# Retention attention and a cosine-gated feed-forward layer on one core: the tile of rows 1024 to 1535 computes its second layer directly, and the seven block products begin one tile later

## The chip, the cores and the metric

The kernel runs on one core of a Trainium2 chip. The metric is the device time of one execution in microseconds (us), lower is better; the time given for a kernel is the median of its runs. A profile is one execution taken by the hardware profiler, and its span reaches from the first to the last instruction.

The core has five engines, each with an instruction stream of its own that it works through in order: PE is TensorE (matmuls; PEld is its weight load), DVE is VectorE, ACT is ScalarE, POOL is GpSimd, SP is SyncE. SP issues nearly all the DMA transfers of this kernel; SPq in a profile is that queue.

## The reference

```python
# q, k, v: (8, 8, 576, 64) float32: batch, head, position, head dimension
scores = scale * np.matmul(q, k.transpose(0, 1, 3, 2))
gamma = 1.0 - 2.0 ** (-5.0 - np.arange(H, dtype=np.float32))
Dmat = np.where(rel >= 0, gamma[:, None, None] ** rel[None, :, :], 0.0)   # rel = i - j
attn = np.matmul(scores * Dmat[None, :, :, :], v)

x = attn.transpose(0, 2, 1, 3).reshape(4608, 512)      # one row per token
h = x @ w_in             # 512 -> 2048
g = h * np.cos(h)
out = g @ w_out          # 2048 -> 512, float32
```

A causal attention without softmax, whose weights decay with the distance, then a two-layer feed-forward block with the activation h·cos(h).

## The kernel before

**Groups and tiles.** The 4608 rows are 36 groups of 128 rows (`NG`), nine to every two batches. The feed-forward layers work on ten tiles: `widths = [512, 256, 256] + [512] * 7`. Tile 0 is rows 0 to 511, tiles 1 and 2 are 256 rows each, tile 3 is rows 1024 to 1535 (groups 8 to 11), tile 9 is the last.

**A group's way.** `load(g)` issues the DMAs of q, k and v on SyncE (tiles fq, fk, fv, five buffers each). `prep(g)` scales q and k by powers of gamma into `qks` and casts v into `vb`: three instructions on GpSimd (lines 140 and 156; for groups above 25 the cast is ScalarE's). `transposes(g)` issues on SyncE a transposing DMA from `qks` to `qkT` (line 167). On TensorE, `scores` makes the products of k and q within the group (line 195), and VectorE multiplies them by the causal mask (line 207). Groups of one batch are tied by a state: `states([g, g+1])` adds their products of k and v (lines 266, 285, 287), and `attn_out` joins the masked scores times v with q times the state (lines 319, 333); ScalarE copies the result into the tile's `xT` (line 350). `scores2(g)` is the scores of g and g+1, in the PSUM banks a and b. `unit(g, ...)` and `unit7(g, ...)` are the states of g+1 and g+2, the output of g and g+1, and, if `more`, `scores2(g+2)`. So a unit asks for `prep` of up to g+3 and for the transposes of g+2 and g+3.

**The first layer.** `mm1` makes one block of 1024 PSUM columns: the matmuls (line 365), the cosine on ScalarE (line 373), the product on VectorE into the bf16 tile `gT` (line 374). A tile of 512 rows has eight blocks, in the banks a, b and m. `gT` has one buffer.

**The second layer, directly.** `mm2` makes 128 rows at a time with 16 matmuls of 128x512 (line 382); ScalarE copies the result (line 392), SyncE stores it. Tiles 0 to 2 do this. `todo` lists which attention work is put in ahead of which matmul.

**The second layer by seven products.** From tile `S7` on, `gT` is taken as two by two blocks (the halves of its rows and of its 16 column tiles), as is `w_out`. Seven products of sums of blocks (112 matmuls of 128x256, line 517) replace eight of blocks. The sums of `w_out` are made once by `w_sums` on VectorE (line 418); those numbered 3 and 4 are made in place in `w_out_sb`, so they can only follow the last direct use of it, and stand in tile `S7`'s first layer. The sums of `gT` are `g_sum` (line 445): sum 5 on VectorE, the others on GpSimd, two column tiles an instruction, with some exceptions in tile `S7` and in the last tile. The products go in the order 3, 4, 5, 2, 1, 7, 6. Products 3 and 4 need no sum of `gT`. `at` says which unit stands ahead of which product, and `late_sums` emits the second half of the sums within the unit ahead of product 4.

**The order of instructions.** It is written by hand: each engine works through its instructions in the order in which the program emits them. What feeds the attention is ordered by `feed(s)`, called with the store of group s of the output (in `mm2` after each 128 rows; in `mm2_seven` after products 5, 2, 7 and 6). `feed` emits `prep`, `transposes` and `load` for later groups. Before tile `S7` it has a loop with these limits:

```python
while prepared < min(loaded, 2 * s + 7, s + 11, starts[S7] // P + 8):
    prep(prepared)
```

From tile `S7` on, with n the tile's number after `S7` and r the store's number in the tile:

```python
while prepared < min(NG, starts[S7] // P + 10 + 4 * n + ((0, 1, 2, 4) if n else (-1, 0, 1, 4))[r]):
    prep_next()
```

With `S7 = 3` this gives, as GpSimd and SyncE get it: groups up to 15 by s = 5; group 16 among the sums of tile 3, group 17 at s = 9, 18 at s = 10, 19 to 21 at s = 11; 22 at s = 13, 23 at s = 14, 24 and 25 at s = 15; and so on, four groups a tile, of which the last two come with its last store.

The functions that the change touches, and what calls them:

Of the kernel before, what the change touches and what calls it, by code (L numbers as in the profile page):

```python
# [17 lines left out]
def kernel(  # L18
# [16 lines left out]
    nc = tc.nc  # L35
    P = 128
# [7 lines left out]
    NG = NTOK // P  # L44
# [9 lines left out]
    assert sum(widths) == NTOK  # L54
    starts = [sum(widths[:n]) for n in range(len(widths))]
    N_PE_T = 6
    S7 = 3
    LD = 5

    consts = ctx.enter_context(tc.tile_pool(name="consts", bufs=1))  # L60
# [70 lines left out]
    def prep(g, early=False, kv_first=False):  # L131

        c = g % PER
        fk, fv = (tiles.pop(("f" + n, g)) for n in "kv")
        qks = nat.tile([P, 2, H, D], BF16, tag="qks", name="qks")
        vb = nat.tile([P, H, D], BF16, tag="vb", name="vb")
        qkT = trp.tile([P, 2 * HG, P], BF16, tag="qkT", name="qkT")

        def scaled(eng, m, f, by):
            eng.tensor_tensor(  # L140
                out=qks[:, m].rearrange("p (b a) d -> p a b d", a=2),
                in0=f.rearrange("p (a b) d -> p a b d", a=2),
                in1=by[:, c, :].rearrange("p (a b) -> p a b", a=2).unsqueeze(3).to_broadcast(
                    [P, 2, HG, D]
                ),
                op=ALU.mult,
            )

        if not early and not kv_first:
            scaled(nc.gpsimd, 0, tiles.pop(("fq", g)), gq)  # L150
        scaled(nc.vector if g == 3 else nc.gpsimd, 1, fk, gk)
        if early:
            tiles["fv", g] = fv
        else:
            copy_v = nc.scalar.copy if g > starts[S7] // P + 17 else nc.gpsimd.tensor_copy
            copy_v(vb, fv)  # L156
            if c == MIX and g > PER:
                copy_v(v_odd[HP:, g // PER % 2], fv[HP:])
        if kv_first:
            scaled(nc.gpsimd, 0, tiles.pop(("fq", g)), gq)  # L160
        qT = qT4[:, :, g * P : (g + 1) * P] if early else qkT[:, :HG, :]
        tiles["a", g] = (qks, vb, qkT, qT)
# [213 lines left out]
    def mm2(n, tsi, et):  # L376
        gT = tiles["g", n]
        if et == 0:
            bank = {0: "nmnm", 1: "nm", 2: "mn"}[n][tsi]
            tiles["o", tsi] = psum.tile([P, DM], F32, tag=bank, name="o")  # L380
        ps = tiles["o", tsi]
        nc.tensor.matmul(  # L382
            ps,
            lhsT=gT[:, et, tsi * P : (tsi + 1) * P],
            rhs=w_out_sb[:, et, :],
            start=(et == 0),
            stop=(et == ET - 1),
        )
        if et == ET - 1:
            s = starts[n] // P + tsi  # L390
            ot = op.tile([P, DM], F32, tag="oabcd"[1 + s % 4], name="ot")
            nc.scalar.copy(ot, ps)  # L392
            nc.sync.dma_start(out[s * P : (s + 1) * P, :], ot)
            feed(s)

    E2 = ET // 2
# [28 lines left out]
    def g_sum(n, x, e0, e1):  # L425

        gT = tiles["g", n]
        a, b, op_ = {
            5: ((0, 0), (0, 1), ALU.add),
            2: ((1, 0), (1, 1), ALU.add),  # L430
            1: ((0, 0), (1, 1), ALU.add),
            7: ((0, 1), (1, 1), ALU.subtract),
            6: ((1, 0), (0, 0), ALU.subtract),
        }[x]
        if ("gs", n, x) not in tiles:
            tiles["gs", n, x] = sump.tile([P, E2, 256], BF16, tag=f"gs{x}", name=f"gs{x}")
        on_dve = x == 5 or (n, x) == (S7, 2) or (n, x, e0) in (
            (S7, 1, 4), (last, 1, 0), (last, 2, 4)
        )
        step = e1 - e0 if on_dve else 2  # L440
        for e in range(e0, e1, step):
            i0, i1 = (
                gT[:, k * E2 + e : k * E2 + e + step, r * 256 : (r + 1) * 256] for r, k in (a, b)
            )
            i = (nc.vector if on_dve else nc.gpsimd).tensor_tensor(  # L445
                out=tiles["gs", n, x][:, e : e + step], in0=i0, in1=i1, op=op_
            )
            if on_dve:
                tiles["gate"] = i
            elif "gate" in tiles:  # L450
                tc.add_manual_dep(
                    i.ins,
                    tiles.pop("gate").ins.name,
                    mybir.DependencyInfo(mybir.DependencyClass.Sync, mybir.DependencyReason.DATA),
                    reason="port free",
                )

    def sums_after(n, i):

        if n == S7:  # L460
            if i < 4:
                w_sums(3 + i % 2, i // 2 * 4, i // 2 * 4 + 4)
            elif i < 6:
                g_sum(n, 5, i % 4 * 4, i % 4 * 4 + 4)
                if i == 5:
                    g_sum(n, 6, 0, 4)
            elif i == 7:
                g_sum(n, 2, 0, E2)
                g_sum(n, 1, 4, E2)
                g_sum(n, 1, 0, 4)  # L470
                for e in (0, 4):
                    g_sum(n, 7, e, e + 4)
                prep_next(kv_first=True)
                g_sum(n, 6, 4, E2)
        elif n == S7 + 1 and i in (3, 7):
            for x in (5, 2, 1):
                g_sum(n, x, i - 3, i + 1)
            for x in (7, 6) if i == 7 else ():
                for e in (0, 4):
                    g_sum(n, x, e, e + 4)  # L480
        elif i == 3:
            for x in (5, 2, 1, 7, 6) if n < last else (5, 1, 2, 7, 6):
                g_sum(n, x, 0, 4)
        elif i == 7 and n == last:
            late_sums(n)
# [113 lines left out]
    def feed(s):  # L599
# [2 lines left out]
        before = loaded  # L602
        n, r = divmod(s - starts[S7] // P, 4)
        if n >= 0:
            while prepared < min(NG, starts[S7] // P + 10 + 4 * n + ((0, 1, 2, 4) if n else (-1, 0, 1, 4))[r]):
                prep_next()
            while transposed < prepared:
                transposes(transposed)
                transposed += 1
            ahead = starts[S7] // P + 14 if n == 0 and r < 3 else prepared + LD  # L610
            while loaded < min(NG, prepared + LD, ahead):
                load(loaded)
                loaded += 1
            return
# [165 lines left out]
    for n, w in enumerate(widths):  # L780
# [8 lines left out]
        else:  # L789
            m = 1024 // w  # L790
            blocks = [(et, 0, w) for et in range(0, ET, m)]
            if n > S7:
                blocks = [(e + k * E2, 0, w) for e in range(0, E2, m) for k in range(2)]
        banks = {0: "abmabmab", 1: "bmba", 2: "bmab", 3: "mamabmab"}.get(n, "abmabmab")
        for i, (et, c0, cw) in enumerate(blocks):
# [27 lines left out]
        elif n == 2:  # L823
            todo = [(11, lambda: scores2(g)), (25, lambda: unit(g, "m", soon=True))]
            late += [lambda: unit(g + 2, "b", False)]
        else:
            at = {}
            if n + 1 < len(widths):
# [1 line left out]
                    4: lambda then, off: unit7(g, "st", True, lambda: late_sums(n), off),  # L830
                    1: lambda then, off: unit7(g + 2, "n", True, then),
                }
                if n in (3, 4):
                    at = {
                        5: lambda then, off: (then(), scores2(g)),
                        1: lambda then, off: unit7(g, "n", True, then),
                        6: lambda then, off: unit7(g + 2, "b", n > 3, then),
                    }
            mm2_seven(n, at)
            continue  # L840
        todo.sort(key=lambda u: u[0])
# [42 lines left out]
```

## Time and profile before

| | us |
|---|---|
| runs | 300.07, 300.51, 303.6 |
| median | 300.51 |
| profiled execution, span | 298.2 |
| tile 3: first layer, second layer | 84.18 to 99.55, 99.55 to 116.78 |
| tile 4: first layer, second layer | 116.78 to 132.53, 132.53 to 149.83 |
| tile 5: first layer, second layer | 149.83 to 163.65, 163.65 to 179.84 |
| tile 6: first layer, second layer | 179.84 to 193.65, 193.65 to 209.19 |

| engine | busy us | share of the span |
|---|---|---|
| PE | 287.1 | 96% |
| POOL | 209.4 | 70% |
| DVE | 207.9 | 70% |
| ACT | 135.9 | 46% |

The layers' limits are TensorE's: the start of the first matmul of line 365 or of line 382 or 517 in its timeline. The profiled execution has no other time than its span; the runs' median lies 2.3 us above it. The granted clock of the core is 1.000. A line of a timeline gives start, length, engine, line, operation, tiles, shape, how many of it were merged (x), and in brackets the engine's idle time ahead of it and what ended that.

### The profile page before, as it was taken

Reading aid. Unit: us, or ns where it says so; the run is one execution under the profiler, and the core shown is the slowest. Engines: PE = TensorE matmul, PEld = TensorE weight load, DVE = VectorE, ACT = ScalarE, POOL = GpSimd, SP = SyncE. Lnnn points to the kernel's source line nnn. Section 1 sums busy time; section 2 is a strip of 40 time slices with the busy share of each in tenths; the row PEclk is TensorE's granted clock in tenths of the full one; section 3 lists DMA queues with packets and bytes.
Section 4 is the critical chain, followed back from the end, with each engine's and each line's share of the span. In section 5 each row is a group of like instructions: output and inputs, shape, how many; then the busy total and the mean of one; then the engine's idle time right before and its main releaser. Section 6 shows DMA issues by size and latency. Waiting matters only on the chain.

```text
span 298.2 us, 7384 instructions
## 1 busy us (share of the span) xinstructions
PE 287.1 (96%) x3113; PEld 195.3 (65%) x3113; DVE 207.9 (70%) x245; ACT 135.9 (46%) x167; POOL 209.4 (70%) x214
## 2 busy tenths in 40 slices
PE   8899999999999999979999999999999999999995
PEld 3478646848578786448744875488448845874584
DVE  5677637564579994788848874887489757935872
ACT  2656433514255432642346554546464446425620
POOL 2750066436445599997999999599959946980693
PEclk9999999999999999999999999999999999999999
DMA  7999999999999999999999997998690260031013
GB/s 203 212 209 206 209 214 213 200 243 208 208 174 222 211 239 213 217 279 176 198 224 229 209 200 183 212 208 201 122 194 2 73 143 0 2 106 36 0 44 99
DMA packets 154304, 50.28 MB, mean 169 GB/s; under 512 B 140832, under 2 KB 153248, under 8 KB 154272
## 3 DMA queue, kind: packets, MB, share of 16 engines
q1 hardware_dynamic: 149504, 45.10, 77.2%
q0 software_dynamic: 4224, 4.19, 8.5%
q8 instruction: 24, 0.39, 0.6%
q10 hardware_dynamic: 544, 0.52, 0.5%
q14 instruction: 8, 0.07, 0.1%
HBM read 36.70 MB, written 9.44 MB: 155 GB/s over the span
## 4 chain that ended last, share of the span: by engine, by line
PE 43%; POOL 25%; SPq 13%; DMA 8%; DVE 5%; issue 3%; ACT 1%; POOLq 0%; DVEq 0%
PE h L365 22%; POOL gs L445 17%; PE o L517 11%; SPq L117 8%; POOL qks L140 6%; PE o L382 5%; SPq L167 4%; DVE gT L374 3%; DMA fk<-in_k_dram 2%; DMA w_in_sb<-in_moe_w_in_dram 2%; DMA qkT<-qks 2%; POOL vb L156 2%; DVE gs L445 2%; DMA fv<-in_v_dram 1%; ACT cosh L373 1%
## 5 line engine op out<-in xcount | busy, mean ns | idle before, releaser
L445 POOL TENSOR_TENSOR gs<-gT 128x512 bf16<-128x512 bf16 x102 | 116.3, 1180 | 29.4 <-DVE gs L445 29.4
L365 PE MATMUL h<-xT,w_in_sb 128*128 128x512 bf16 (+2 forms) x832 | 127.6, 313 | 2.6 <-DVE gT L374 1.8
L374 DVE TENSOR_TENSOR gT<-h,cosh 128x1024 bf16<-128x1024 f32 x72 | 87.8, 1223 | 43.7 <-ACT cosh L373 40.7
L373 ACT ACTIVATE cosh<-h,half_pi 128x1024 f32<-128x1024 f32 x72 | 80.2, 1114 | 72.2 <-PE h L365 69.8
L365 PEld LDWEIGHTS <-w_in_sb 128*128 128x128 bf16 x832 | 75.9, 98 | 51.6 <-issue 3.0
L140 POOL TENSOR_TENSOR qks<-fq,gq 128x512 bf16<-128x512 f32 x32 | 34.0, 1062 | 40.9 <-DMA fq<-in_q_dram 40.9
L517 PEld LDWEIGHTS <-gs 128*128 128x128 bf16 x576 | 53.6, 98 | 10.1 <-POOL gs L445 2.9
L140 POOL TENSOR_TENSOR qks<-fk,gk 128x512 bf16<-128x512 f32 x35 | 37.3, 1066 | 8.0 <-DMA fk<-in_k_dram 7.4
L207 DVE TENSOR_TENSOR ret<-sc,tri 128x1024 bf16<-128x1024 f32 x32 | 38.1, 1217 | 2.8 <-PE sc L195 2.7
L517 PE MATMUL o<-ws,gs 128*128 128x256 bf16 (+1 forms) x352 | 39.1, 268 | 0.7 <-POOL gs L445 0.5
L382 PE MATMUL o<-w_out_sb,gT 128*128 128x512 bf16 x128 | 30.1, 380 | 0.0
L517 PE MATMUL o<-w_out_sb,gT 128*128 128x256 bf16 x224 | 26.6, 273 | 0.1
L517 PE MATMUL o<-w_out_sb,gs 128*128 128x256 bf16 x224 | 26.1, 273 | 0.5 <-POOL gs L445 0.4
L537 DVE TENSOR_TENSOR ot<-o,ot 128x512 f32<-128x512 f32 (+2 forms) x25 | 14.9, 603 | 14.7 <-PE o L517 14.5
L517 PEld LDWEIGHTS <-gT 128*128 128x128 bf16 x224 | 21.4, 98 | 4.7 <-DVE gT L374 0.7
L350 ACT CAST xT<-ov 128x1024 bf16<-128x1024 f32 (+1 forms) x18 | 16.5, 917 | 16.1 <-PE ov L319 13.9
L445 DVE TENSOR_TENSOR gs<-gT 128x1024 bf16<-128x1024 bf16 (+1 forms) x18 | 20.4, 1148 | 0.3
L382 PEld LDWEIGHTS <-gT 128*128 128x128 bf16 x128 | 11.8, 98 | 12.5
L156 POOL CAST vb<-fv 128x512 bf16<-128x512 f32 x22 | 14.3, 651 | 4.4 <-DMA fv<-in_v_dram 4.2
L564 ACT COPY ot<-o 128x512 f32<-128x512 f32 x7 | 4.1, 586 | 20.5 <-PE o L517 20.5
L392 ACT COPY ot<-o 128x512 f32<-128x512 f32 x8 | 4.7, 588 | 17.4 <-PE o L382 17.4
L537 DVE TENSOR_TENSOR ot<-ot,o 128x512 f32<-128x512 f32 x14 | 9.6, 684 | 4.0 <-ACT ot L569 2.4
(70 smaller groups left out, 175.8 us busy)
## 6 DMA issues: line engine op xcount, KB each, us to landing
out_dram<-ot SPq DMA_DIRECT2D x35, 256.0 KB, 4.0
fk<-in_k_dram SPq DMA_DIRECT2D x32, 256.0 KB, 5.2
fv<-in_v_dram SPq DMA_DIRECT2D x32, 256.0 KB, 5.2
fq<-in_q_dram SPq DMA_DIRECT2D x30, 256.0 KB, 4.5
w_in_sb<-in_moe_w_in_dram POOLq DMA_DIRECT2D x4, 512.0 KB, 8.9
w_out_sb<-in_moe_w_out_dram POOLq DMA_DIRECT2D x4, 512.0 KB, 16.2
fq<-in_q_dram SPq DMA_DIRECT2D x8, 128.0 KB, 4.0
fk<-in_k_dram SPq DMA_DIRECT2D x8, 128.0 KB, 4.4
```

The costliest lines, as they stand in the source:

```text
L117: i = nc.sync.dma_start(f[p0:p1], src[b, :, s0 : s0 + p1 - p0, :].rearrange("h s d -> s h d"))
L140: eng.tensor_tensor(out=qks[:, m].rearrange("p (b a) d -> p a b d", a=2), in0=f.rearrange("p (a b) d -> p a b d", a=2), in1=by[:, c, :].re ...
L156: copy_v(vb, fv)
L207: nc.vector.tensor_tensor(out=ret.rearrange("p a b i -> p (a b) i"), in0=ps.rearrange("p a b i -> p (a b) i"), in1=mask.unsqueeze(1).to_br ...
L350: evac(tiles["x", n][:, :, t0 : t0 + len(gs) * P], ps.rearrange("p c x i -> p c (x i)"))
L365: nc.tensor.matmul(ps[:, j, :], lhsT=w_in_sb[:, dg, (et + j) * P : (et + j + 1) * P], rhs=xT[:, dg, c0 : c0 + w], start=(dg == 0), stop=(d ...
L373: nc.scalar.activation(cosh, ps, ACTF.Sin, bias=half_pi, scale=1.0)
L374: nc.vector.tensor_mul(gT[:, et : et + m, c0 : c0 + w], ps, cosh)
L382: nc.tensor.matmul(ps, lhsT=gT[:, et, tsi * P : (tsi + 1) * P], rhs=w_out_sb[:, et, :], start=(et == 0), stop=(et == ET - 1),)
L445: i = (nc.vector if on_dve else nc.gpsimd).tensor_tensor(out=tiles["gs", n, x][:, e : e + step], in0=i0, in1=i1, op=op_)
L517: nc.tensor.matmul(dst[i], lhsT=lhs[:, e, j * P : (j + 1) * P], rhs=rhs[:, e, c0:c1], start=(x in (3, 4, 1, 7) and e == 0 and (i == 0 or l ...
L537: pend.append(lambda: nc.vector.tensor_tensor(out=out_, in0=in0, in1=in1, op=op_))
```

## The change

`S7` goes from 3 to 4: tile 3 computes its second layer with `mm2`, and tile 4 is the first with seven products. What was written for the first two tiles of seven products (own places for the sums, some of them on VectorE; units ahead of products 5, 1 and 6; one group's `prep` among the sums; limits on `prepared` and `loaded`) is taken out, and tile 4 gets the order that tiles 5 to 8 have. Tile 3 gets a `todo` list: `scores2(12)` ahead of matmul 4, unit 12 ahead of matmul 24, unit 14, with the scores of groups 16 and 17, ahead of matmul 46 of its 64.

```diff
-    S7 = 3
+    S7 = 4
...
-            copy_v = nc.scalar.copy if g > starts[S7] // P + 17 else nc.gpsimd.tensor_copy
+            copy_v = nc.scalar.copy if g > 25 else nc.gpsimd.tensor_copy
...
     def mm2(n, tsi, et):
-            bank = {0: "nmnm", 1: "nm", 2: "mn"}[n][tsi]
+            bank = {0: "nmnm", 1: "nm", 2: "mn", 3: ("n", "st", "n", "st")}[n][tsi]
...
     def g_sum(n, x, e0, e1):
-        on_dve = x == 5 or (n, x) == (S7, 2) or (n, x, e0) in (
-            (S7, 1, 4), (last, 1, 0), (last, 2, 4)
-        )
+        on_dve = x == 5 or (n, x, e0) in ((last, 1, 0), (last, 2, 4))
...
     def sums_after(n, i):
-        if n == S7:
-            if i < 4:
-                w_sums(3 + i % 2, i // 2 * 4, i // 2 * 4 + 4)
-            elif i < 6:
-                g_sum(n, 5, i % 4 * 4, i % 4 * 4 + 4)
-                if i == 5:
-                    g_sum(n, 6, 0, 4)
-            elif i == 7:
-                g_sum(n, 2, 0, E2)
-                g_sum(n, 1, 4, E2)
-                g_sum(n, 1, 0, 4)
-                for e in (0, 4):
-                    g_sum(n, 7, e, e + 4)
-                prep_next(kv_first=True)
-                g_sum(n, 6, 4, E2)
-        elif n == S7 + 1 and i in (3, 7):
-            for x in (5, 2, 1):
-                g_sum(n, x, i - 3, i + 1)
-            for x in (7, 6) if i == 7 else ():
-                for e in (0, 4):
-                    g_sum(n, x, e, e + 4)
-        elif i == 3:
+        if n == S7 and i < 4:
+            w_sums(3 + i % 2, i // 2 * 4, i // 2 * 4 + 4)
+        if i == 3:
             for x in (5, 2, 1, 7, 6) if n < last else (5, 1, 2, 7, 6):
                 g_sum(n, x, 0, 4)
...
     def feed(s):
-            while prepared < min(NG, starts[S7] // P + 10 + 4 * n + ((0, 1, 2, 4) if n else (-1, 0, 1, 4))[r]):
+            while prepared < min(NG, starts[S7] // P + 10 + 4 * n + (0, 1, 2, 4)[r]):
                 prep_next()
             while transposed < prepared:
                 transposes(transposed)
                 transposed += 1
-            ahead = starts[S7] // P + 14 if n == 0 and r < 3 else prepared + LD
-            while loaded < min(NG, prepared + LD, ahead):
+            while loaded < min(NG, prepared + LD):
                 load(loaded)
...
-            if n > S7:
+            if n >= S7:
                 blocks = [(e + k * E2, 0, w) for e in range(0, E2, m) for k in range(2)]
...
+        elif n == 3:
+            todo = [
+                (4, lambda: scores2(g)), (24, lambda: unit7(g, "b")), (46, lambda: unit7(g + 2, "b"))
+            ]
         else:
             at = {}
             if n + 1 < len(widths):
                 at = {
                     4: lambda then, off: unit7(g, "st", True, lambda: late_sums(n), off),
                     1: lambda then, off: unit7(g + 2, "n", True, then),
                 }
-                if n in (3, 4):
-                    at = {
-                        5: lambda then, off: (then(), scores2(g)),
-                        1: lambda then, off: unit7(g, "n", True, then),
-                        6: lambda then, off: unit7(g + 2, "b", n > 3, then),
-                    }
             mm2_seven(n, at)
```

In tile n the name g in these lists is the first group of tile n+1: 12 in tile 3, 16 in tile 4. The limits of `feed` move with `starts[S7]`, which goes from 1024 to 1536.

## The prediction

> **What bounds the kernel now.** I read the page first, then TensorE's timeline tile by tile, then the windows of each layer, then GpSimd's and SyncE's timelines to see what stands in front of what. Numbers: tile 3 is the tile of rows 1024 to 1535, tile 4 the next; "group g" is the 128 rows from 128g on, that is the scaled q, k and the cast v which `prep(g)` makes on GpSimd.
>
> ```profile
> PE 287.1 (96%) x3113; PEld 195.3 (65%) x3113; DVE 207.9 (70%) x245; ACT 135.9 (46%) x167; POOL 209.4 (70%) x214
> L445 POOL TENSOR_TENSOR gs<-gT 128x512 bf16<-128x512 bf16 x102 | 116.3, 1180 | 29.4 <-DVE gs L445 29.4
> ```
>
> TensorE is busy for 96% of the span, so a tile costs what its matmuls cost unless something that they need is late. The windows (span, then busy time and count of PE, PEld, DVE, ACT, POOL) show where it is late now:
>
> ```profile
> 99.55:116.78 17.23, 16.57 (x274) 13.42 (x272) 14.31 (x19) 6.12 (x10) 15.35 (x15) 1.00 1.20 244
> 116.78:132.53 15.75, 13.97 (x66) 6.26 (x64) 11.72 (x9) 7.80 (x7) 15.12 (x18) 1.00 1.26 243
> 132.53:149.83 17.30, 16.58 (x289) 13.73 (x288) 13.95 (x17) 5.82 (x9) 15.58 (x15) 1.00 0.97 188
> ...
> 179.84:193.65 13.81, 13.81 (x66) 6.27 (x64) 9.02 (x9) 7.80 (x7) 10.73 (x12) 1.00 0.93 190
> 193.65:209.19 15.54, 15.54 (x257) 13.32 (x256) 11.97 (x15) 8.57 (x14) 15.54 (x14) 1.00 0.90 199
> ```
>
> The last two are tile 6, first and second layer, with no gap: 13.81 + 15.54 = 29.35 us is the price of an undisturbed tile of seven products. The first three are tile 3's second layer and both layers of tile 4. Tile 4 takes 15.75 + 17.30 = 33.05 us, 3.7 more than tile 6 (it has 0.55 us more scores; the rest is gaps). Tile 5 takes 179.84 - 149.83 = 30.01, 0.66 more. These gaps are all that can be won.
>
> GpSimd's timeline shows the order that counts:
>
> ```profile
> 123.92 1.03 POOL L140 TENSOR_TENSOR qks<-fq,gq 128x512 bf16<-128x512 f32 x1
> 124.92 1.03 POOL L140 TENSOR_TENSOR qks<-fk,gk 128x512 bf16<-128x512 f32 x1
> 125.91 0.60 POOL L156 CAST vb<-fv 128x512 bf16<-128x512 f32 x1
> 126.48 1.03 POOL L140 TENSOR_TENSOR qks<-fq,gq 128x512 bf16<-128x512 f32 x1
> 127.48 1.03 POOL L140 TENSOR_TENSOR qks<-fk,gk 128x512 bf16<-128x512 f32 x1
> 128.47 0.60 POOL L156 CAST vb<-fv 128x512 bf16<-128x512 f32 x1
> 129.70 4.49 POOL L445 TENSOR_TENSOR gs<-gT 128x512 bf16<-128x512 bf16 x4 [0.63 <-DVE gs L445]
> 135.91 13.42 POOL L445 TENSOR_TENSOR gs<-gT 128x512 bf16<-128x512 bf16 x12 [1.72 <-DVE gs L445]
> 149.27 1.06 POOL L140 TENSOR_TENSOR qks<-fq,gq 128x512 bf16<-128x512 f32 x1
> ...
> 190.21 18.32 POOL L445 TENSOR_TENSOR gs<-gT 128x512 bf16<-128x512 bf16 x16 [3.08 <-DVE gs L445]
> ```
>
> The first six lines are groups 20 and 21: they run **before** tile 4's sixteen sums (129.70 to 149.3). A group takes 2.56 us. In tile 6 the sums are one block of 18.3 us that starts 190.21 - 179.84 = 10.4 us after the tile.
>
> **Tile 3, second layer.** Removed: 112 matmuls at 5.35/48 = 0.1115 us (the chain has "PE o L517 x48" at 5.35), 12.5 us; ten GpSimd sums of 1.18; four DVE sums and six DVE additions; three ACT copies. Added: 64 matmuls of 128x512 at 0.216 (the chain has 45 in 9.71), 13.8 us, and four ACT copies of 0.59, which lie beside the matmuls (ACT is busy 6.12 of 17.23 there). Attention: one `scores2`, 0.55, and two units of 1.61 (165.49 to 167.10 on TensorE). Bare sum 13.82 + 0.55 + 3.22 = 17.6. Four stores of 256 KB stay four.
>
> Two waits come in. **First**, `scores2(12)` now stands after four matmuls, and its second half writes bank b, which the first layer's last block holds. That block's last matmul group ends at 99.72, its cosine at 100.9, its product on DVE (1.23) at 102.15; TensorE gets there at 99.55 + 0.86 + 0.28 = 100.7. Price 1.5 us; from 0 (DVE early) to 1.9 (today's product ends at 102.56). I take 1.5. **Second**, unit 14 now also makes the scores of groups 16 and 17, so their transposed copies are needed some 20 us sooner. SyncE works through its queue in order and lies behind: the store of group 6 goes out at 105.38 though its matmuls were done at about 79. Behind it now stand the transpose of 16 (1.3), the three loads of group 18 (3.1, as at 106.50 to 109.53), the store of group 7 (1.0), then the transpose of 17: issue at about 111.9, landing 4.1 later (median of that stretch), 116.0. TensorE: 102.15 + 0.28 + 20 x 0.216 + 1.61 + 22 x 0.216 + 0.96 + 0.28 = 114.4. Price 1.6; from 0 to 4.0 (landing 6.5, the slowest of all transposes). I take 1.6. Groups 16 and 17 themselves are no limit: the last load of 17 is issued at 104.37 and lands 4.8 later, and GpSimd, without sums, needs 0.6 after it. So the layer takes 17.6 + 1.5 + 1.6 = 20.7 against 17.23: **+3.4**, and tile 4 starts at S = 120.2.
>
> **Tile 4, first layer.** Today it waits 1.78 us for a product on DVE, which stood behind one DVE sum of 3.33 us that ran while GpSimd worked through groups 20 and 21. In the new order GpSimd is idle then, so 13.81: **-1.9**. The four `w_sums` (0.68 to 0.94 us of DVE) move in from tile 3: per block DVE has 1.23 + 0.7 against TensorE's 1.73, 0.2 behind per block; three double banks hide it for TensorE, but the sums start some 0.5 later, at S + 10.9. If that cover is gone, 0.5 is the price.
>
> **Tile 4, second layer: the step that decides.** `feed` is called with the store that follows product 5. For s = 8 to 11 (tile 3) the old-style branch now stops at group starts[4]/128 + 8 = 20, so groups 16 to 19 are made there, and groups 20 and 21 only at s = 12, in tile 4's second layer. The later tiles' order has put all sixteen sums of tile 4 on GpSimd by then: eight after block 3, eight in `late_sums`, called from the unit ahead of product 4. GpSimd takes its work in order, so group 20 begins at S + 10.9 + 18.3 = S + 29.2: q, k by 31.2, v by 31.8. SyncE then starts the transpose of 20 at S + 31.2 and of 21 (k at 29.2 + 2.56 + 2.0) at S + 33.8.
>
> But unit 18, ahead of product 1, asks for `states([19, 20])` and `scores2(20)`. TensorE reaches it at S + 22.6 (in tile 6: 202.43 - 179.84). It waits until 31.8: 9.2 us. Then states and output of group 18, 19 (0.96), and another wait for the transpose of 21: 33.8 + 3.1 = S + 36.9 (3.1 is the shortest landing, right where the DMA queue has nothing else; SyncE itself is blocked on that transpose). The rest is half the scores and products 1, 7, 6: 0.27 + 5.25. Tile 5 would start at S + 42.4, not S + 29.35: 13.0 us of waiting. Behind the waiting TensorE stand the products, so the additions on DVE and two stores; nobody outside this tile asks for them. Bounds of the 13.0: 9.2 (the transposes land before the states are through, in which case group 20's v alone decides) to 16.4 (landing 6.5).
>
> **The array's clock after a hole.** No row of before shows matmuls after a long idle spell; the granted clock is 1.00 in every window. At the start of the span the 14 idle-filling matmuls are slow:
>
> ```profile
> 1.26 5.32 PE L185 MATMUL idle<-zeros 128*128 128x512 bf16 x14 [1.26 <-DVE zeros L662]
> 6.42 1.04 PE L708 MATMUL tr<-ident,qs 128*128 128x128 bf16 x8
> ```
>
> 14 in 5.16 us where 0.216 each would be 3.0: 2.1 lost. After the gap of 1.78 us in tile 4 nothing is lost (8 matmuls in 1.89). A hole of 9 us is nearer to the start than to 1.8, so I take 2.1, from 0 to 4.2 (both holes).
>
> The Trainium skill ("TensorE: Matmul & The Clock Gate", Part 1) has the same from the other side and speaks against this change: an idle window of some 3.4 us halves the array's rate, and about 3.4 us of work restores it. As an estimate from that page the loss is 1.7 instead of 2.1, and the forecast would be 0.4 us lower; the start of this trace agrees with halving (0.43 us apiece for ten matmuls).
>
> Second layer of tile 4: 42.4 + 2.1 - 13.8 = 30.7 against 17.30: **+13.4**.
>
> **Tile 5.** Six groups (20 to 25, 16.0 us with the extra cast) now run between the sums of tile 4 and of tile 5, to S + 45.2; tile 5 starts at S + 44.5 and wants its sums 10.4 later, so nothing waits, and today's 0.66 of gaps goes: **-0.7**. From tile 6 on both kernels have the same order.
>
> **Sum.** 3.4 - 1.9 + 13.4 - 0.7 = +14.2 on the profiled execution, whose span is 298.2 (312.4 after). The runs' median is 300.51, 2.3 above that span; I keep that offset: 300.5 + 14.2 = **314.7 us**.
>
> **Rivals.**
> *Faster or level: GpSimd keeps up.* If group 20 and 21 reach GpSimd ahead of tile 4's sums, tile 4's second layer is tile 6's 15.54 (-1.8), and the sum is 3.4 - 1.9 - 1.8 - 0.7 = -1.0: **299.5**, and 296.5 without the two waits of tile 3. For it: ten sums fewer on an engine with 17% of the chain. Against it: the order of calls, and GpSimd and TensorE are in order. It decides at one point: whether group 20 is done by S + 22.6.
> *The late groups hurt one tile later.* If tile 4 runs on, the six groups push tile 5's sums to S + 45.2, the tenth sum ends at S + 56.7, and 7.4 us follow (172.48 to 179.84): tile 6 at S + 64.1 = 184.3 against 179.84, **305.0**. Against it: it also needs tile 4 not to ask for group 20.
> *The transposes are slow as well.* Landings of 6.5 at both places and a slow array after both holes: 2.4 + 3.4 + about 1 more, **321**.
>
> **How the numbers follow.** Forecast 0.79, GpSimd keeps up 0.05, one tile later 0.06, slow transposes 0.10. The forecast's own range takes off the clock, and both waits of tile 3 (2.1 + 3.1: 309.5) and adds the transposes' upper ends in part: 309.5 to 318.5. The range for 8 in 10 is 309 to 319. 2% of the time, about what a measurement of this kernel can tell from no change, is 6 us, so the line is 306.5: slower 0.90 (forecast, slow transposes, the upper edge of the 305 case), within 2% 0.085, faster by over 2% 0.015.
>
> **What would show it.** Right: on GpSimd groups 20 and 21 directly behind sixteen sums; on TensorE an idle 9 us ahead of the states before product 1 of tile 4, released by GpSimd, and 3 to 4 us ahead of the second scores there, released by a transpose; matmuls after it at 0.2 us or more where 0.11 is normal; no gap in tile 4's first layer. Wrong: no hole at that place, or a tile 3 whose second layer takes under 18 or over 23 us.

## The result and the profile after

| | before | after |
|---|---|---|
| median of the runs (four each), us | 300.61 | 319.06 |
| lowest, highest | 300.07, 303.6 | 318.5, 319.81 |
| ratio to before | | 1.0635, 95% interval 1.0603 to 1.0667 |
| profiled execution: time, span | span 298.2 | 319.14, span 317.4 |

The change makes the kernel 6.35% slower by the ratio of the runs: 18.5 us by the medians, 19.2 by the two profiled spans. The forecast was +14.2 us, 314.7, with a range of 309 to 319. The windows of the kernel after (span, then busy time and count of PE, PEld, DVE, ACT, POOL, then granted clock, DMA share, GB/s), one for each layer of tiles 3, 4 and 5:

```profile
100.73:124.81 24.08, 19.11 (x252) 9.83 (x255) 10.61 (x12) 6.11 (x10) 11.32 (x13) 0.93 1.20 227
124.81:138.63 13.82, 13.77 (x65) 6.23 (x65) 10.27 (x12) 8.38 (x8) 2.98 (x3) 1.00 1.21 234
138.63:169.62 30.99, 19.29 (x258) 15.40 (x257) 12.63 (x15) 5.81 (x9) 30.63 (x32) 0.78 0.62 114
169.62:183.43 13.81, 13.71 (x64) 6.27 (x64) 9.02 (x9) 7.80 (x7) 4.26 (x6) 1.00 1.28 219
183.43:199.05 15.62, 15.62 (x273) 13.58 (x272) 12.93 (x16) 8.19 (x14) 15.62 (x14) 1.00 0.87 197
```

Two windows are long: tile 3's second layer, 24.08 where it was 17.23, and tile 4's, 30.99 where it was 17.30. In both the granted clock is below 1. In the third, GpSimd is busy for 30.63 of 30.99 us while TensorE works for 19.29. From tile 6 on nothing is lost: from there to the end are 118.4 us in both kernels.

GpSimd's timeline in tile 4, after:

```profile
135.65 18.29 POOL L443 TENSOR_TENSOR gs<-gT 128x512 bf16<-128x512 bf16 x16 [11.35 <-DVE gs L443]
153.89 1.05 POOL L140 TENSOR_TENSOR qks<-fq,gq 128x512 bf16<-128x512 f32 x1
154.89 1.05 POOL L140 TENSOR_TENSOR qks<-fk,gk 128x512 bf16<-128x512 f32 x1
155.88 0.62 POOL L156 CAST vb<-fv 128x512 bf16<-128x512 f32 x1
156.44 1.05 POOL L140 TENSOR_TENSOR qks<-fq,gq 128x512 bf16<-128x512 f32 x1
```

Sixteen sums, and behind them group 20 (q, k, v) and group 21. Ahead of the sums GpSimd idles for 11.35 us. TensorE's timeline, ahead of and behind product 1 of tile 4:

```profile
147.88 0.32 PE L266 MATMUL st<-vb,qks 128*64 128x64 bf16 x8
156.54 0.42 PE L266 MATMUL st<-vb,qks 128*64 128x64 bf16 x8 [8.34 <-POOL vb L156]
156.73 1.09 PE L333 MATMUL ov<-ret,vb 128*64 128x128 bf16 x16
157.75 0.43 PE L319 MATMUL ov<-qkT,sb 64*64 64x128 bf16 x8
160.51 0.64 PE L195 MATMUL sc<-qkT 64*64 64x128 bf16 x16 [2.33 <-DMA qkT<-qks]
161.76 0.64 PE L195 MATMUL sc<-qkT 64*64 64x128 bf16 x16 [0.61 <-DMA qkT<-qks]
162.33 7.45 PE L496 MATMUL o<-ws,gs 128*128 128x256 bf16 x48
169.62 13.98 PE L365 MATMUL h<-xT,w_in_sb 128*128 128x512 bf16 x62
```

The state of group 19 is made, that of group 20 waits 8.34 us for its v; then the scores wait for the two transposes; then 48 matmuls take 7.3 us (162.33 to 169.62), where tile 6 of the kernel before has 5.25. In tile 3:

```profile
115.70 0.39 PE L195 MATMUL sc<-qkT 64*64 64x128 bf16 x16
119.17 0.64 PE L195 MATMUL sc<-qkT 64*64 64x128 bf16 x16 [3.08 <-DMA qkT<-qks]
120.14 4.83 PE L382 MATMUL o<-w_out_sb,gT 128*128 128x512 bf16 x17 [0.33 <-issue]
```

The scores of group 16, a wait of 3.08 us for the transpose of group 17, and matmuls that run slower behind it. The windows cut where the granted clock changes (the clock is the third figure from the end):

```profile
118.74:122.16 3.42, 2.66 (x21) 1.29 (x23) 1.23 (x1) 0.59 (x1) 0.52 (x1) 0.50 1.07 226
122.16:152.88 30.72, 25.58 (x220) 14.92 (x219) 17.62 (x19) 12.58 (x14) 19.35 (x19) 1.00 0.83 160
152.88:166.53 13.65, 7.04 (x84) 5.17 (x85) 4.45 (x6) 1.62 (x3) 13.51 (x16) 0.50 0.73 123
```

### The profile page after: what moved, and what is told of

Its sections match the earlier page's. It is cut to its first block, busy times and chain, and to the rows that moved or that the text cites. A ratio compares the mean times of both kernels' runs of the same rounds, so it can differ in the third digit from the quotient of the medians.

```text
span 317.4 us, 7243 instructions
## 1 busy us (share of the span) xinstructions
PE 291.2 (92%) x3040; PEld 193.6 (61%) x3065; DVE 198.2 (62%) x235; ACT 136.4 (43%) x168; POOL 197.2 (62%) x204
## 2 busy tenths in 40 slices
DMA packets 153792, 50.28 MB, mean 158 GB/s; under 512 B 140832, under 2 KB 152224, under 8 KB 153760
## 4 chain that ended last, share of the span: by engine, by line
PE 64%; POOL 13%; DMA 9%; SPq 6%; issue 4%; ACT 1%; DVE 1%; POOLq 0%; DVEq 0%
PE h L365 34%; PE o L496 15%; POOL gs L443 11%; PE o L382 8%; SPq L117 5%; DMA qkT<-qks 4%; PE sc L195 2%; POOL qks L140 2%; DMA fq<-in_q_dram 2%; DMA fk<-in_k_dram 2%; DMA fv<-in_v_dram 2%; PE ov L333 2%; ACT cosh L373 1%; PE ov L319 1%; PE st L266 1%
## 5 line engine op out<-in xcount | busy, mean ns | idle before, releaser
L443 POOL TENSOR_TENSOR gs<-gT 128x512 bf16<-128x512 bf16 x92 | 105.4, 1187 | 46.1 <-DVE gs L443 46.1
L496 PEld LDWEIGHTS <-gs 128*128 128x128 bf16 x496 | 47.4, 100 | 8.9 <-POOL gs L443 1.8
L382 PE MATMUL o<-w_out_sb,gT 128*128 128x512 bf16 x180 | 43.7, 386 | 1.1 <-issue 0.7
L496 PE MATMUL o<-ws,gs 128*128 128x256 bf16 (+1 forms) x304 | 34.9, 277 | 0.3 <-POOL gs L443 0.2
L382 PEld LDWEIGHTS <-gT 128*128 128x128 bf16 x192 | 18.1, 99 | 20.4 <-issue 1.8
L496 PE MATMUL o<-w_out_sb,gs 128*128 128x256 bf16 x192 | 22.4, 273 | 0.5 <-POOL gs L443 0.4
L496 PE MATMUL o<-w_out_sb,gT 128*128 128x256 bf16 x192 | 22.8, 273 | 0.0
L496 PEld LDWEIGHTS <-gT 128*128 128x128 bf16 x192 | 18.4, 98 | 3.8
L392 ACT COPY ot<-o 128x512 f32<-128x512 f32 x12 | 7.1, 588 | 30.7 <-PE o L382 30.7
L195 PE MATMUL sc<-qkT 64*64 64x128 bf16 (+1 forms) x480 | 11.8, 227 | 8.5 <-DMA qkT<-qks 7.2
L156 POOL CAST vb<-fv 128x512 bf16<-128x512 f32 x22 | 13.7, 621 | 8.1 <-DMA fv<-in_v_dram 7.6
L195 PEld LDWEIGHTS <-qkT 64*64 64x64 bf16 (+1 forms) x512 | 9.5, 110 | 13.5 <-DMA qkT<-qks 8.0
L287 DVE TENSOR_TENSOR s<-st,s 128x256 f32<-128x256 f32 x18 | 7.6, 422 | 14.7 <-PE st L266 10.9
```

The lines of the kernel that those rows point to most:

```text
L195: nc.tensor.matmul(ps[i0:i1, he, hg, :], lhsT=qkT[d0 : d0 + D, HG + hg, i0:i1], rhs=qT[d0 : d0 + D, hg, :], start=True, stop=True,)
L382: nc.tensor.matmul(ps, lhsT=gT[:, et, tsi * P : (tsi + 1) * P], rhs=w_out_sb[:, et, :], start=(et == 0), stop=(et == ET - 1),)
L443: i = (nc.vector if on_dve else nc.gpsimd).tensor_tensor(out=tiles["gs", n, x][:, e : e + step], in0=i0, in1=i1, op=op_)
L496: nc.tensor.matmul(dst[i], lhsT=lhs[:, e, j * P : (j + 1) * P], rhs=rhs[:, e, c0:c1], start=(x in (3, 4, 1, 7) and e == 0 and (i == 0 or l ...
```

## The experiments

The theory: the time goes to three places that each had a term in the sum, namely GpSimd's order in tile 4 (the hole ahead of product 1), SyncE's order in tile 3 (the transpose of group 17), and half a clock behind either hole. The rivals: GpSimd has too much work in any order; the DMA traffic sets when the transpose lands; the slow matmuls are slow for another reason. In every kernel below the sums of `gT` in tile 4, but for sum 5, are on GpSimd if nothing else is said. The kernels ran at different times and on different chips, each beside the kernel before; a ratio is to the kernel before of the same stretch of measurements.

### Groups 20 and 21 ahead of tile 4's sums

```diff
-            while prepared < min(loaded, 2 * s + 7, s + 11, starts[S7] // P + 8):
+            while prepared < min(loaded, 2 * s + 7, s + 11, starts[S7] // P + 10):
```

> Change: the limit of the old-style branch of feed is two groups higher, so groups 20 and 21 are prepared at s = 10 and 11, ahead of tile 4's sums on GpSimd. Nothing else. Theory A (TensorE's hole in tile 4 comes from groups 20 and 21 standing behind sixteen sums): the 8.3, 2.3 and 0.6 us holes ahead of product 1 go, and with them the slow clock after them; tile 4 takes 29.4 instead of 44.8 us, time 319.1 - 15.4 = 303.7 us, between 303 and 305; tile 3 is as after. Rival B (GpSimd has too much to do in this stage, whatever the order: six groups and 32 sums in tiles 4 and 5): the wait moves to a product that needs a sum, in tile 4 or 5, and at least 5 of the 15 us stay, time 308 or more.

Measured: 304.62 us, ratio 1.013 (1.0095 to 1.0164), as theory A has it. One limit moved by two groups gives back 14.4 of the 18.5 us. On GpSimd group 21 ends at 133.8, ahead of the sums:

```profile
130.60 1.04 POOL L140 TENSOR_TENSOR qks<-fq,gq 128x512 bf16<-128x512 f32 x1 [2.18 <-DMA fq<-in_q_dram]
131.71 1.04 POOL L140 TENSOR_TENSOR qks<-fk,gk 128x512 bf16<-128x512 f32 x1
132.87 0.90 POOL L156 CAST vb<-fv 128x512 bf16<-128x512 f32 x1
135.71 18.30 POOL L443 TENSOR_TENSOR gs<-gT 128x512 bf16<-128x512 bf16 x16 [1.95 <-DVE gs L443]
```

Tile 4 takes 154.68 - 123.64 = 31.0 us instead of 44.8. Of the 1.7 us that it has over 29.35, 1.1 are in the first layer, most of it TensorE's waits for products on VectorE (0.33 and 0.45 in the timeline), whose `w_sums` now run beside groups 20 and 21, and 0.6 in the second, where it waits for a sum. Rival B is out: the work was the same, only the order changed.

### Unit 14 of tile 3 ahead of matmul 60

```diff
-                (4, lambda: scores2(g)), (24, lambda: unit7(g, "b")), (46, lambda: unit7(g + 2, "b"))
+                (4, lambda: scores2(g)), (24, lambda: unit7(g, "b")), (60, lambda: unit7(g + 2, "b"))
```

> Change: in tile 3 unit 14 (with the scores of groups 16 and 17) stands ahead of matmul 60 instead of 46. Theory A (the 3.1 us wait there is for the transpose of group 17, which SyncE issues at a time that TensorE does not set; the matmuls after it run slowly because of the hole): 14 matmuls fill the hole, the wait goes, the slow stretch after it (about 1.5 us) goes too, tile 4 starts 4 to 4.7 us sooner, time 314.4 to 315. Rival B (the wait is for something in the unit itself, its banks or its states): the wait moves along with the unit, time unchanged at 319. Rival C (no slow clock after a 3 us hole): 316.

Measured: 313.9 us, ratio 1.0443 (1.0412 to 1.0474): 5.2 us less than after, and half a us less than theory A had. In the profile tile 3's second layer takes 19.78 us (100.12 to 119.90) instead of 24.08, the slow stretch included. Fourteen matmuls fill the hole; the scores of group 17 find their transpose:

```profile
118.10 0.39 PE L195 MATMUL sc<-qkT 64*64 64x128 bf16 x16
118.67 0.42 PE L195 MATMUL sc<-qkT 64*64 64x128 bf16 x16 [0.18 <-DVE s L287]
```

### scores2(12) later, so that bank b is free

```diff
-                (4, lambda: scores2(g)), (24, ...
+                (11, lambda: scores2(g)), (24, ...
```

> Change: in tile 3 scores2(12) stands ahead of matmul 11 instead of 4, so bank b is free when TensorE comes. Theory A: the 1.4 us wait for VectorE's last product goes, but the transpose of group 17 lands when it lands, so the wait for it grows by the same 1.4 us: time unchanged, 319.1 within 0.6, the wait for the transpose 4.5 us instead of 3.1. Rival B (waits in a row on TensorE add up): 317.7.

Measured: 319.64 us, ratio 1.0644 (1.0628 to 1.0661), no change. The wait for bank b is gone (1.25 us of idle in the timeline after), and the wait for the transpose grew by more than that:

```profile
118.75 0.64 PE L195 MATMUL sc<-qkT 64*64 64x128 bf16 x16 [4.87 <-DMA qkT<-qks]
```

The transpose landed at 118.7, 18.7 us after the layer's start, where it was 18.4 in the profile after. (It was issued sooner, at 113.1 instead of 114.9, and took 5.6 us to land instead of 4.2.) Taking away a wait ahead of the landing on TensorE only made the wait for it longer; rival B's 317.7 is below all four runs (319.39 to 320.16).

### The holes filled with matmuls that nobody reads

```diff
     def scores2(g, put_off=None):
+            fill = {16: (0, 14), 20: (10, 2)}.get(g, (0, 0))
-            scores(g, "a", parts=2)
-            scores(g + 1, "b", parts=2, put_off=put_off)
+            scores(g, "a", fill[0], parts=2)
+            scores(g + 1, "b", fill[1], parts=2, put_off=put_off)
...
     def unit7(g, bank, more=True, then=lambda: None, put_off=None):
+        if g == 18:
+            warm(psum.tile([P, 512], F32, tag="m", name="idle"), 38)
```

> Change: matmuls of zeros that nobody reads fill TensorE's holes: 14 ahead of the scores of group 17, 38 ahead of the states of 19 and 20, 10 and 2 ahead of the scores of 20 and 21. All waits stay. Theory A (the array runs at a lower rate for some us after a hole): products 1, 7, 6 of tile 4 take 5.3 instead of 7.3 us and the matmuls of tile 3 after the hole lose their 1.5; 64 more matmuls make the kernel 3 to 3.5 us faster, 315.6 to 316. Rival B (these matmuls are slow for another reason, such as GpSimd or the DMA at work beside them): no faster, 319 or some tenths more.

Measured: 315.56 us, ratio 1.0508 (1.0483 to 1.0533): 64 useless matmuls make the kernel 3.5 us faster. What TensorE waits for comes as late as before; the granted clock is 1.00 throughout, and the 48 matmuls of products 1, 7 and 6 take 5.25 us again (161.10 to 166.35):

```profile
160.75 0.42 PE L195 MATMUL sc<-qkT 64*64 64x128 bf16 x16 [1.04 <-DMA qkT<-qks]
161.10 5.41 PE L496 MATMUL o<-ws,gs 128*128 128x256 bf16 x48
```

So 3.5 of the 18.5 us were half clock behind holes: tile 3's second layer takes 22.8 us (100.99 to 123.81) instead of 24.1, tile 4's 28.7 (137.62 to 166.35) instead of 31.0.

### The kernel before, once more

> The kernel before, unchanged, profiled once more, to see how far single stages scatter between executions. Theory A (tile 3's second layer starts at 99.5 to 101 us in any kernel with this front part; the 1.2 us between the two first profiles is scatter in when a transpose of tile 2 lands): a start that differs from 99.55 by some tenths, up to 1.5. Rival B (the changed order delays tile 2): 99.5 again, while all changed kernels were at 99.5 to 101.

Measured: one execution of 300.39 us, span 298.7, tile 3's second layer from 100.44. Rival B is out. Over all fourteen profiles that layer starts between 99.22 and 100.99 whatever the change. The 1.2 us between the first two profiles is scatter, and may be why the spans differ by 19.2 us and the medians by 18.5.

### The transpose of group 17 ahead of the loads of group 18

```diff
+            ahead = s + 11 + (s == 6)
-            while prepared < min(loaded, 2 * s + 7, s + 11, starts[S7] // P + 8):
+            while prepared < min(loaded, 2 * s + 7, ahead, starts[S7] // P + 8):
...
-            if N_PE_T <= transposed < min(prepared, s + 11) and (
+            if N_PE_T <= transposed < min(prepared, ahead) and (
```

> Change: on top of the changed kernel, feed may prepare and transpose one group more at s = 6, so on SyncE the transpose of group 17 stands ahead of the loads of group 18 and the store of group 7. Theory A (the transpose is late since it stands behind these transfers in SyncE's queue): it is issued when k of group 17 is ready, at about 111.2, and lands at 115.3 to 116 instead of 119.1; the wait in tile 3 is under 0.7 us, no stretch at half clock follows it, tile 4 starts 4 to 4.7 us sooner: 314.4 to 315. Rival B (the DMA engines' traffic sets the landing, whatever the order): it lands at 118 or later, 318 us.

Measured: 313.8 us, ratio 1.0488 (1.045 to 1.0526), 5.3 us less than after by the medians. The kernel before ran faster beside these runs (298.97) than beside those with the later unit (300.25), so by the ratios the gain is somewhat smaller than there. In the profiles the two agree: tile 3's second layer takes 19.99 us here (100.30 to 120.29). SyncE's queue, first after, then here, from the store of group 6 on:

```profile
107.41 1.08 SPq L393 DMA_DIRECT2D out_dram<-ot  x1
108.60 1.46 SPq L167 DMA_TRANSPOSE qkT<-qks  x1
110.12 1.67 SPq L117 DMA_DIRECT2D fq<-in_q_dram  x1
111.84 0.87 SPq L117 DMA_DIRECT2D fk<-in_k_dram  x1
112.75 0.91 SPq L117 DMA_DIRECT2D fv<-in_v_dram  x1
113.76 1.03 SPq L393 DMA_DIRECT2D out_dram<-ot  x1
114.90 1.30 SPq L167 DMA_TRANSPOSE qkT<-qks  x1
```

```profile
105.95 1.08 SPq L393 DMA_DIRECT2D out_dram<-ot  x1
107.14 4.96 SPq L167 DMA_TRANSPOSE qkT<-qks  x2
112.15 0.58 SPq L117 DMA_DIRECT2D fq<-in_q_dram  x1
```

After, the transpose of 17 leaves 7.5 us behind that store and lands at 119.1; here both transposes stand directly behind it, the second leaves at 109.9 (sooner than the 111.2 expected) and lands at 113.6. TensorE's wait for it is gone:

```profile
116.05 0.42 PE L195 MATMUL sc<-qkT 64*64 64x128 bf16 x16 [0.18 <-DVE s L287]
```

The queue's order was the cause. Of the 5.5 us by which the transpose lands sooner, 3.5 are its place in the queue, 0.5 a quicker landing (3.7 us instead of 4.2), and 1.5 the store itself, which goes out earlier in this profile, within its scatter. The DMA share of tile 3's second layer is 1.20 after and 1.19 here; between that store and the landing it is 1.27 (107.41 to 119.10) and 1.14 (105.95 to 113.60), so lighter traffic can account for some of the 0.5 us at most.

### The three together

```diff
-            while prepared < min(loaded, 2 * s + 7, s + 11, starts[S7] // P + 8):
+            while prepared < min(loaded, 2 * s + 7, s + 11, starts[S7] // P + 10):
...
-                (4, lambda: scores2(g)), (24, lambda: unit7(g, "b")), (46, lambda: unit7(g + 2, "b"))
+                (11, lambda: scores2(g)), (24, lambda: unit7(g, "b")), (60, lambda: unit7(g + 2, "b"))
```

> Change: the early groups 20 and 21, unit 14 ahead of matmul 60, and scores2(12) ahead of matmul 11, together. Theory A (each wait removed uncovers the next: the loads of group 21 land at 133 to 134 whatever TensorE does, so GpSimd can't begin tile 4's sums before about 134, though tile 4 now starts at 120.2 and wants them at 131): some 2.5 us of wait for the sums at product 2, time 302 to 303. Rival B (gains add up: 304.6 less 4.7): 300.

Measured: 303.89 us, ratio 1.0142 (1.01 to 1.0183), nothing gained over the early groups alone, and 0.9 us above the upper end of theory A. Tile 4 starts 3.8 us sooner than there (119.85 against 123.64), but GpSimd ends group 21 at 134.3 where it was 133.8, since its load lands then, and sixteen sums follow. The wait is now for a sum, at product 2, as theory A had it; the 3.41 us at half the clock that follow it (146.34 to 149.75) are what it left out:

```profile
144.84 0.61 PE L496 MATMUL o<-w_out_sb,gs 128*128 128x256 bf16 x4 [2.67 <-POOL gs L443]
```

### Groups 20 and 21 between the halves of the sums

On top of the early transpose of 17 and the later `scores2(12)`:

```diff
     def sums_after(n, i):
                 g_sum(n, x, 0, 4)
+            if n == S7:
+                prep_two()          # prep and transposes of groups 20 and 21
...
-        on_dve = x == 5 or (n, x, e0) in
+        on_dve = x == 5 or (n, x) == (S7, 2) or (n, x, e0) in
```

> Change: the transpose of group 17 early, scores2(12) ahead of matmul 11, groups 20 and 21 between the first and the second half of tile 4's sums with their transposes at once, and sum 2 of tile 4 on VectorE, so 12 instead of 16 sums on GpSimd there. Theory A (GpSimd then has twelve sums and two groups, 18.9 us, from S + 10.9, and TensorE wants the last sum at S + 28): tile 4 without a hole over 2 us, tile 5 starts at about 149.6 against 149.8 before: 299.5 to 301.5, level with before. Rival B (VectorE can't take the sum besides its own work while GpSimd runs): 303 or more. Rival C (the gain of relieving GpSimd of ten sums shows at last): below 298.

Measured: 303.38 us, ratio 1.0128 (1.0088 to 1.0168): theory A missed, and the number is rival B's. The groups are ready when the states ask for them, but k of group 20 is done at 139.92 on GpSimd, its transpose leaves SyncE at 140.12, directly behind the loads of group 23, and lands 5.8 us later; half a clock follows. The expectation had left out what the transposes take. For VectorE TensorE waits 0.68 us in this profile, so rival B's cause is there, but small:

```profile
145.95 0.52 PE L195 MATMUL sc<-qkT 64*64 64x128 bf16 x16 [2.18 <-DMA qkT<-qks]
```

A kernel that also asks for groups 20 and 21 later, ahead of product 6, and has ten sums left on GpSimd:

> Change: as e7_mid, and in tile 4 unit 18 (states of 19 and 20, scores of 20 and 21) stands ahead of product 6 instead of 1, and the second half of sum 1 goes to VectorE: ten sums and two groups for GpSimd. Theory A (what is left in e7_mid is the wait for the transposes of 20 and 21 and the half clock after it; asked for 5 us later they are there, and GpSimd is done 2.3 us sooner): tile 4 takes 30 to 31 us instead of 35.1, tile 5 starts at 148.5 to 150, time 299 to 300.5, level with before or up to 0.5% faster. Rival B (the two groups among the sums cost GpSimd and VectorE more than their own time): 302 or more.

Measured: 302.13 us, ratio 1.0071 (1.0043 to 1.01). Tile 4 takes 32.8 us (118.67 to 151.46) where 30 to 31 was expected: the transposes are no longer waited for, but 2.13 us are, for VectorE at product 2. VectorE's three sums take 1.5 us apiece where one takes 0.64 at 128.97, and GpSimd's q and k of group 20 beside them some 1.5 us each instead of 1.04:

```profile
135.98 4.52 DVE L443 TENSOR_TENSOR gs<-gT 128x1024 bf16<-128x1024 bf16 x3
142.28 1.91 PE L498 MATMUL o<-w_out_sb,gs 128*128 128x256 bf16 x16 [2.13 <-DVE ot L540]
```

This is rival B, in number and in cause. The expectation was again too low by about 2 us.

### The direct tile alone, tile 4 as in the kernel before

```diff
+                if n == S7:      # tile 4's units ahead of products 5, 1 and 6, its sums after
+                    at = {5: ..., 1: ..., 6: ...}      # blocks 3 and 7, as in the kernel before
...
-                (4, lambda: scores2(g)), ..., (46, lambda: unit7(g + 2, "b"))
+                (11, lambda: scores2(g)), ..., (46, lambda: unit7(g + 2, "b", False))
```

with groups 20 and 21 at s = 10 and 11.

> Change: the direct second layer of tile 3 alone: tile 4 has the order that the kernel before gives it (sums after blocks 3 and 7, scores2(16) ahead of product 5, unit 16 ahead of product 1, unit 18 ahead of product 6), groups 20 and 21 are prepared at s = 10 and 11, scores2(12) ahead of matmul 11; no scores of groups 16 and 17 in tile 3. Theory A (the relief of ten sums buys nothing, since tile 4's sums wait for groups 20 and 21, which come at the pace of SyncE's loads): no wait in tile 3, tile 4 starts at 117, GpSimd ends group 21 at about 134.5 and the sixteen sums at 153, tile 5 starts at 153 to 153.5 against 149.8: 303 to 304. Rival B (the direct tile is worth the 1 to 4 us that its removed gaps promise): 297 to 299.5.

Measured: 301.91 us, ratio 1.0068 (1.0044 to 1.0092), between the two. No wait over 0.8 us is left in tiles 3 and 4, and the ten sums that GpSimd was spared are not to be found in the time. GpSimd waits for group 21's load and only then begins:

```profile
129.88 1.04 POOL L140 TENSOR_TENSOR qks<-fq,gq 128x512 bf16<-128x512 f32 x1 [2.07 <-DMA fq<-in_q_dram]
131.00 1.04 POOL L140 TENSOR_TENSOR qks<-fk,gk 128x512 bf16<-128x512 f32 x1
132.16 0.61 POOL L156 CAST vb<-fv 128x512 bf16<-128x512 f32 x1
132.73 18.30 POOL L443 TENSOR_TENSOR gs<-gT 128x512 bf16<-128x512 bf16 x16
```

The kernel before begins tile 4's sums at 129.70: sooner, with ten sums more behind it. The change relieves GpSimd in a stretch in which it waits for loads.

Last, the same with sum 2 of tile 4 on VectorE, and then also the second half of sum 1:

```diff
-        on_dve = x == 5 or (n, x, e0) in ((last, 1, 0), (last, 2, 4))
+        on_dve = x == 5 or (n, x) == (S7, 2) or (n, x, e0) in ((last, 1, 0), (last, 2, 4))
```

> Change: as e9_direct_alone, and sum 2 of tile 4 on VectorE, so GpSimd has twelve sums there instead of sixteen. Theory A (what keeps e9 1.7 us above the kernel before is that GpSimd begins the sums only after group 21, at 132.7, and needs 18.3 us for them): four sums fewer end 4.6 us sooner, the waits of 0.5 each for sums go, tile 5 starts at 149.5 to 150 instead of 151.5, time 300 to 300.6, level with before. Rival B (VectorE becomes late in its place): 301.5 to 303.

> Change: as e10_direct_sum2, and the second half of sum 1 of tile 4 on VectorE too (ten sums on GpSimd). Theory A: with GpSimd out of the way TensorE's own work sets tile 4, 30.8 us from 117.1 with the wait of the first layer: tile 5 at 148 to 149.5, time 298.8 to 300, up to 0.5% below the kernel before. Rival B (VectorE, which runs its bf16 sums slowly beside GpSimd, is late): 301 or more.

Measured: 299.77 us, ratio 0.9995 (0.9974 to 1.0016), and 299.76 us, ratio 0.9998 (0.9978 to 1.0018). Both are level with the kernel before, so no version found beats it. The first came out as theory A had it; the second lies within theory A's range, but not below the first. In the second, tile 3's second layer and tile 4 together take 50.31 us (99.22 to 149.53); in the kernel before they take 50.28. TensorE pays 1.3 us more for 64 matmuls than for 112 smaller ones, and still waits for VectorE in tile 4's first layer:

```profile
130.70 1.89 PE L365 MATMUL h<-xT,w_in_sb 128*128 128x512 bf16 x8 [1.32 <-DVE gT L374]
```

## What the prediction had right, and where it fell short

**Right: the step that decides.** With S the start of tile 4 (120.2 predicted, 124.81 measured):

| in tile 4 | predicted | measured |
|---|---|---|
| first layer | 13.81 | 13.82 |
| GpSimd's sums begin, end | S + 10.9, 29.2 | S + 10.8, 29.1 |
| v of group 20 ready | S + 31.8 | S + 31.7 |
| transpose of group 21 lands | S + 36.9 | S + 36.9 |
| half clock, products 1, 7, 6 | 2.1 | 2.0 |
| second layer | 30.7 | 31.0 |
| tile 5 | 29.35 | 29.4 |

The landing of group 21 is 161.72 on the trace. Most of this could be read from the order in which three in-order queues get their work and from durations of tile 6. The first experiment shows the cause: with the two groups ahead of the sums, 14.4 us come back. Two things fit better than the working deserves. The wait for a transpose was forecast ahead of the second scores, 3 to 4 us; it came ahead of the first (2.33 us, the transpose of 20, which the sum left out) and only 0.61 ahead of the second, and the landing of 21 alone set the end. And the half clock was priced from slow matmuls at the start of the span: that 2.1 met 2.0 is in part luck, since behind the same hole these 48 matmuls take 6.68 to 7.68 us in the kernels with `scores2(12)` later, with unit 14 later and with the transpose of 17 first, that is 1.4 to 2.4 above 5.25.

**Wrong: tile 3's second layer, +3.4 predicted, +6.9 measured (24.08 against 17.23).** The prediction itself had named over 23 us there as a sign of being wrong. The step that failed is the one called the second wait, priced 1.6, together with what follows it. Its mechanism held (two experiments take the wait away, one by moving the unit, one by moving the transpose). Its size was off in two ways:

- The transpose of 17 landed 18.4 us after the layer's start (119.1 less 100.73), where 16.45 was counted (116.0 less 99.55): 1.9 us. The store of group 6 was put at 105.38, from the one profile shown; over the fourteen profiles it goes out between 105.1 and 107.4, and the transpose of 17 leaves 7.1 to 7.6 us behind it in the kernels that keep this queue order and have the transpose of 16 in it, where 6.5 was counted. From issue to landing it took 4.2 us where 4.1 was counted; over the profiles of the changed kernels that can differ too, 5.7 in the last three.
- Half a clock was priced for tile 4 alone, though the same paragraph gave a bound for both holes. The 3 us hole in tile 3 cost another 1.5: from the scores of 17 to tile 4 are 5.64 us (119.17 to 124.81) where 0.28 + 18 x 0.216 = 4.17 was counted.

1.9 + 1.5 are the 3.4 by which that layer was too low. What TensorE does ahead of the landing adds nothing to it: the first wait was 1.25 us where 1.5 was counted, and the scores of group 15 come some 0.5 us later than counted (scores and what follows start at 108.93 and 110.00, 1.07 apart instead of 0.55), but such time only shortens or lengthens the wait for the transpose, as the experiment with `scores2(12)` shows. By layers the 19.2 us between the two spans are 1.2 at the start of tile 3's second layer, 6.9 in it, -1.9 and 13.7 in tile 4, and -0.6 in tile 5; 0, 3.4, -1.9, 13.4 and -0.7 were forecast. The 1.2 is scatter, as the kernel before shows, run once more. In the other direction, the runs' median lies 1.7 us above the span after, where the 2.3 of the kernel before was kept.

**The rivals.** Faster or level: out; the point it named, group 20 done by S + 22.6, was missed by 9 us. The relief of GpSimd that spoke for it is real (105.4 us of sums instead of 116.3) and stands where GpSimd waits for loads. Later by one tile: in the kernel with the groups ahead of the sums tile 5 takes 29.8 us (154.68 to 184.50), no more than the 30.0 before. Slow transposes, 321: its number is nearer to the 319.06 measured than the forecast's 314.7, and it had the half clock behind both holes, but its cause did not come: landings were not slow (4.2 us for the transpose of 17, 3.2 for 21), the transpose of 17 was issued late. With a landing of 6.5 as the only upper end, the issue time was taken as known.

## What to carry to other kernels

When a stage is moved by one step in a program of in-order queues, list for each queue what now stands ahead of the first thing that the moved stage asks for. Here one limit in a feeding loop, two groups too low, cost 14 us, and the ten instructions saved on the same engine bought nothing in any version measured: where they were saved, that engine was waiting for loads. A wait on TensorE of more than 2 us can have a second price behind it, here up to 1.7 us for each 3.41 us at half the clock, and an issue time read from one profile of a queue that lags needs a range of its own.

## What was not expected of the hardware

The granted clock falls to exactly 0.50 behind the holes and stays there for 3.42 us in tile 3 and 13.65 us in tile 4 of the kernel after, 6.83 and 17.07 in the kernel with `scores2(12)` later, and 17.06 in the one with unit 14 later: one, four, two, five and five times 3.41 us. The Trainium skill ("TensorE: Matmul & The Clock Gate", Part 1) has a free-running window of that length, and these stretches agree with it: the penalty comes in whole windows.

The prediction quoted an idle window of some 3.4 us as what halves the rate; here a shorter hole was enough. In the three together, waits of 2.67 and 0.50 us at product 2 were followed by a stretch at half rate from 146.34 to 149.75, and in the kernel with the two groups between the halves of the sums, a wait of 2.18 us by one from 146.12 to 149.53, while a single wait of 2.13 us, in the profile of the kernel with unit 18 ahead of product 6, was not (clock 1.00 around it), nor was the 1.78 us of the kernel before. Executions of one kernel differ in this too. With the early groups three of four have a mean granted clock of 0.994 and take 304.6 to 305.1 us, the fourth 1.000 and 302.7 us. With unit 18 ahead of product 6, two of six have 0.997 and 0.998 and take 300.9 and 301.1 us, the other four 0.992 to 0.994 and 301.6 to 303.1 us: the profile is one of the faster two. That such a hole costs a window in one execution and not in the next would fit a window that runs free of the kernel; no profile here shows two executions of one changed kernel.

The windows of four of the stretches, two in the kernel with `scores2(12)` later, then one of the three together and one with the groups between the halves:

```profile
115.93:122.76 6.83, 3.67 (x24) 1.64 (x26) 1.23 (x1) 0.59 (x1) 3.14 (x4) 0.50 1.17 222
150.06:167.13 17.07, 7.58 (x87) 5.53 (x88) 4.59 (x6) 1.62 (x3) 16.93 (x20) 0.50 0.60 109
146.34:149.75 3.41, 3.41 (x78) 2.71 (x76) 2.28 (x4) 1.85 (x4) 3.41 (x4) 0.50 1.35 228
146.12:149.53 3.41, 3.13 (x43) 2.10 (x36) 2.36 (x2) 0.00 (x0) 3.41 (x4) 0.50 1.09 237
```
